# Attention head of a fused attention and SwiGLU kernel: the fourth key block and the tails moved forward, batch 1's casts and batch 0's check moved between engines

## The chip, the cores and the metric

The kernel runs on one core of a Trainium2 chip. The core has five engines that work side by side, each in its own program order: TensorE (matrix products, PE in the profile, with its weight loads as PEld), VectorE (DVE), ScalarE (ACT), GpSimd (POOL) and SyncE (SP), which here only issues transfers. They wait for one another through semaphores. Matrix products land in PSUM, a small memory of eight banks; everything else lives in SBUF. Transfers run on 16 DMA engines and are issued from the queues of SP, ACT and POOL.

The metric is the device time of one execution in microseconds (us): the median over runs. Beside it there is one profiled execution, whose span runs from its first instruction to its last.

## The reference

Eight batches of eight heads, 576 positions, 64 numbers per head. Attention is causal, with a decay that is a cumulative sum; its output is turned into 4608 rows of 512 and goes through RMS norm and a SwiGLU feed-forward with 1536 hidden columns.

```python
s_pos = np.maximum(s, 0.0)
cum = np.cumsum(s_pos, axis=-1)
bias = -(cum[:, :, :, None] - cum[:, :, None, :])
scores = np.where(causal, -1000000000.0, scale * q @ k.T + np.minimum(bias, 0.0))
attn = softmax(scores)                     # exp(scores - max), divided by the sum
x = (attn @ v).transpose(0, 2, 1, 3).reshape(4608, 512)

xn = x / sqrt(mean(x * x) + 1e-6) * rms_g
g = xn @ w_gate
out = (g * sigmoid(g) * (xn @ w_val)) @ w_out
```

## The kernel before

**Banded attention.** The decay is so strong that a query sees only its own block of 128 keys and the block before it; the rest falls under a bound. The kernel computes that band and checks on the side that this was allowed: check_mag (L368) takes the magnitudes of a batch's cast K or Q into `mag`, check_max (L373) folds them in two halves into a running maximum `acc`. At the very end these and other bounds give a flag; a slow general path stands behind the flag and isn't entered with this data.

**Stages of attention, per batch b.** Names in brackets are used later.

- K and Q come in as fp32 into `kq32` (load_kq L123, and load_kq_tail L129 for positions 512 to 575, the "tail"). w is 0 for K and 1 for Q. They are cast to bf16 into `kqn` (cast L135; quarter r of the positions, quarter 4 is the tail). From batch 2 on other ways are used as well.
- t_step (L180) transposes one head pair hp of K or Q on TensorE, four products into a PSUM tile, and copies it to `kqT` by ScalarE or VectorE. tail_step (L194) does the tails of all head pairs.
- s_step (L225) makes scores of key block kb (0 to 4) for the four heads of group g (0 or 1): S(kb, g), or S(b, kb, g). Four products on TensorE, four exponentials on ScalarE (L274) into a slot of `E`, and a causal mask on GpSimd (L283). Block 3 also needs the tail's queries, block 4 the tail alone, for all heads at once.
- av_step (L292) makes AV(qb, g), the output of query block qb: products on TensorE (L300, L306), division by the sum on VectorE (L313, L315), and with g = 1 the sum of squares, on ScalarE (L321) where `act` is set, else on VectorE (L325), then the RMS scale on GpSimd (L328, L331).
- x_scale (L335, instruction L338, VectorE) applies the scale; xt_step (L352) transposes the block on TensorE (L357) and copies it into `xnT` (L364 ScalarE, L366 VectorE). Most later blocks are transposed by DMA instead.

**Feed-forward.** ffn (L658) takes a chunk c of 512 rows, nine in all. Its loop over fb (12 times) does the gate product Gp (L668), the tanh T on ScalarE (L671), the value product Vp (L677), U = (T + 1) * Gp (L680) and Ht = U * Vp (L673; the last one L685) on VectorE. Then come four blocks of 12 output products each (L690). psF is a ring of four PSUM banks that Gp and Vp, some transposes, the score pairs pairF and the output products share; psS, psAV and psT are single tiles.

**Order.** The whole program is written out in order, each engine runs its own part of it strictly in that order, and there are two ways in which the order is made:

- The head (L773 to L884) is written by hand: all of batch 0's attention but its last query block, up to the transposes of its first 512 rows, which make chunk 0. warm(n) (L593) puts n products in that nothing uses.
- From chunk 0 on, step (L599) is called at fixed places of ffn (a slot, counted in `slot`): after each Gp and each Vp, and among the output products. In each slot it puts in at most one piece from each of the side queues (`act_side`, `v_side`, `pool_side`, `dve_side`), then a score step, or a transpose, an AV and a K/Q transpose, as far as lags counted in slots since the pieces that they need allow it (can_t L530, can_s L542, can_av L561). So the order doesn't depend on times; a piece whose data is late makes its engine wait. In chunk 0 the slots hold batch 1's casts, its transposes of K and Q (do_t L489), batch 0's last block, and batch 1's scores and outputs. During the output products of chunk 0 the query blocks (1,1) to (1,3) of batch 1 are finished; (1,3) is transposed on TensorE before chunk 1 begins.

The lines that the change touches: `when` in check (L421) says in which slots batch 0's check runs; do_t (L496) which engine copies batch 1's transposes; L784 clears the part of the E slots that S(3, g) doesn't write; L828 to L880 are the hand-written order of the head; L881 to L884 batch 0's check of Q; L886 to L894 the queues with batch 1's casts; L903 the queue with batch 0's check of K.

Of the kernel before, what the change touches and what calls it, by code (L numbers as in the profile page):

```python
# [26 lines left out]
def kernel(  # L27
# [12 lines left out]
    nc = tc.nc  # L40
# [340 lines left out]
    slot = [0]  # L381
    first, chunk = [0], [0]
    done = {}
# [34 lines left out]
    def check(b, ws=(1, 0)):  # L418
        t = slot[0] + (8 if b >= KB else 0)

        def when(w):  # L421
            if b < 2:
                return slot[0] % 2 and chunk[0] == b
            return phase() >= 25 and slot[0] >= t and (w == 0 or ready(0, "cast", b, 1))
        dve_side.extend((lambda w=w: when(w), f) for w in (ws if b < KB else (0, 1)) for f in (
            lambda w=w: check_mag(b, w), lambda: check_max(0), lambda: check_max(1),
            lambda w=w: done.__setitem__(("check", b, w), slot[0])))
# [61 lines left out]
    def do_t(key, **kw):  # L489
# [5 lines left out]
        else:  # L495
            if b == 1:  # L496
                kw["dve"] = w == 1 and hp > 1
# [273 lines left out]
    with tc.manual_schedule():  # L771
# [12 lines left out]
        nc.gpsimd.memset(E[:, 6:8, :, 192:256], 0.0)  # L784
# [45 lines left out]
        s_first(1, 0, pairF())  # L830
        load_w(moe_w_val, wv_sb, 0)
# [5 lines left out]
        for w in (0, 1):  # L837
            cast(POOL, 0, w, 4, 5)
# [3 lines left out]
        s_first(0, 1, pairF())  # L842
        do_av((0, 1, 0), psT32())
        s_first(1, 1)
        tail_step(0)
        done["T", 0] = 0
        load_v(0, 4)
        do_av((0, 2, 0))
        s_first(2, 1, pairF())
        s30 = do_s((0, 3, 0))  # L850
        s30(False)
        s31 = do_s((0, 3, 1), pairF())
        s31(False)
        do_av((0, 0, 1), psT32())

# [4 lines left out]
        s30.mask()  # L860
        s31.mask()
        do_av((0, 1, 1), act=True)
        do_av((0, 2, 1), psT32(), act=True)
        warm(4)
        x_scale(0, 0)
        do_av((0, 3, 0))
# [14 lines left out]
        check_mag(0, 1)  # L881
        check_max(0)
        check_max(1)
        done["check", 0, 1] = 0  # L884

        def done_cast(w):  # L886
            done["cast", 1, w] = slot[0]
        later(act_side, 1, [lambda r=r: cast(ACT, 1, 0, r, r + 1) for r in range(4)])
        later(pool_side, 1, [lambda: cast(POOL, 1, 0, 4, 5)])
        later(pool_side, 3, [lambda: done_cast(0)])  # L890
        later(pool_side, 4, [lambda: cast(POOL, 1, 1, 2, 3),
                             lambda: (cast(POOL, 1, 1, 3, 4), done_cast(1)),
                             lambda: cast(POOL, 1, 1, 4, 5)])
        later(dve_side, 3, [lambda r=r: cast(DVE, 1, 1, r, r + 1) for r in (0, 1)])  # L894
# [8 lines left out]
        check(0, (0,))  # L903
# [195 lines left out]
```

## Time and profile before

| | us |
|---|---|
| median of three runs (375.37, 375.38, 375.68) | 375.38 |
| profiled execution, whole | 374.85 |
| its span | 373.2 |
| TensorE busy in it | 347.1 (93%) |
| VectorE busy | 279.6 (75%) |
| ScalarE busy | 240.0 (64%) |
| GpSimd busy | 175.2 (47%) |
| first gate product of chunk 0 starts at | 31.85 |
| first gate product of chunk 1 starts at | 76.10 |

How to read what is quoted from the profile: in a timeline, a row has the start and length in us, the engine, the line of the kernel, the operation, what it writes and reads with shapes, how many instructions the row holds, and in brackets how long the engine stood idle before it and what ended that. A row of waits has engine, tile and line, what it waited for, and then us in total, times, longest. A row of windows has the stretch, its length, then for each engine the busy time and in brackets the instructions, then the granted TensorE clock (1.00 is full speed), the busy share of the DMA engines and GB/s. Lengths of neighbouring instructions on one engine overlap a little, so the distance from start to start is up to 0.1 us shorter than the length.

### The profile page before, as it was taken

Reading aid. Unit: us, or ns where it says so; the run is one execution under the profiler, and the core shown is the slowest. Engines: PE = TensorE matmul, PEld = TensorE weight load, DVE = VectorE, ACT = ScalarE, POOL = GpSimd, SP = SyncE. Lnnn points to the kernel's source line nnn. Section 1 sums busy time; section 2 is a strip of 40 time slices with the busy share of each in tenths; the row PEclk is TensorE's granted clock in tenths of the full one; section 3 lists DMA queues with packets and bytes.
Section 4 is the critical chain, followed back from the end, with each engine's and each line's share of the span. In section 5 each row is a group of like instructions: output and inputs, shape, how many; then the busy total and the mean of one; then the engine's idle time right before and its main releaser. Section 6 shows DMA issues by size and latency. Waiting matters only on the chain. (4 is left out here: it accounts for less than half of the span.)

```text
span 373.2 us, 6936 instructions
## 1 busy us (share of the span) xinstructions
PE 347.1 (93%) x2356; PEld 161.4 (43%) x2356; DVE 279.6 (75%) x525; ACT 240.0 (64%) x626; POOL 175.2 (47%) x277
## 2 busy tenths in 40 slices
PE   1777899899999999899999999999999999999993
PEld 1443444454444444444444444444444444444441
DVE  6778988589887878788889897795488548837730
ACT  3787787547877597776778776777677644323321
POOL 5866734974846565779856825523322310000000
PEclk9879999999999999999999999999999999999998
DMA  7999999799997599959999997973310230020012
GB/s 228 192 206 262 148 208 210 122 201 222 127 204 104 52 200 161 159 56 204 147 166 223 139 118 151 122 56 44 99 23 14 44 105 3 0 84 31 0 42 78
DMA packets 125626, 46.22 MB, mean 124 GB/s; under 512 B 104912, under 2 KB 120784, under 8 KB 125584
## 3 DMA queue, kind: packets, MB, share of 16 engines
q0 software_dynamic: 59920, 11.80, 43.9%
q1 hardware_dynamic: 53040, 24.33, 34.7%
q10 hardware_dynamic: 12624, 9.59, 10.2%
q8 instruction: 20, 0.33, 0.4%
q14 instruction: 22, 0.18, 0.2%
HBM read 38.16 MB, written 9.44 MB: 128 GB/s over the span
## 5 line engine op out<-in xcount | busy, mean ns | idle before, releaser
L274 ACT ACTIVATE E<-psS,biasK 128x256 bf16<-128x256 f32 (+3 forms) x352 | 115.1, 416 | 19.7 <-PE psS L250 18.0
L668 PE MATMUL psF<-xnT,wg_sb 128*128 128x512 bf16 x432 | 111.1, 379 | 1.9 <-DMA xnT<-xs_sb 0.8
L677 PE MATMUL psF<-xnT,wv_sb 128*128 128x512 bf16 x432 | 111.1, 379 | 0.1
L690 PE MATMUL psF<-wout_sb,Ht 128*128 128x512 bf16 x432 | 102.3, 379 | 0.0
L283 POOL TENSOR_SCALAR_AFFINE_SELECT E<-E 128x512 bf16<-128x512 bf16 x72 | 51.9, 721 | 92.8 <-ACT E L274 92.0
L671 ACT ACTIVATE T<-psF 128x512 f32<-128x512 f32 x108 | 64.4, 598 | 41.5 <-PE psF L668 38.3
L680 DVE SCALAR_TENSOR_TENSOR U<-T,psF 128x512 bf16<-128x512 f32 x108 | 73.6, 682 | 21.8 <-ACT T L671 21.8
L673 DVE TENSOR_TENSOR Ht<-U,psF 128x512 bf16<-128x512 bf16 x99 | 67.7, 684 | 7.5 <-PE psS L250 0.5
L668 PEld LDWEIGHTS <-wg_sb 128*128 128x128 bf16 x432 | 38.7, 98 | 46.3 <-issue 7.5
L677 PEld LDWEIGHTS <-wv_sb 128*128 128x128 bf16 x432 | 38.6, 98 | 42.8 <-issue 4.6
L690 PEld LDWEIGHTS <-Ht 128*128 128x128 bf16 x432 | 38.7, 98 | 42.0 <-issue 2.3
L338 DVE SCALAR_TENSOR_TENSOR xs_sb<-x_sb,al_all,g_row 128x512 bf16<-128x512 bf16 (+1 forms) x40 | 32.4, 810 | 16.6 <-POOL al_all L331 15.0
L695 ACT ACTIVATE osb<-psF 128x512 f32<-128x512 f32 x36 | 21.4, 595 | 33.7 <-PE psF L690 29.3
L321 ACT ACTIVATE xs_sb<-x_sb 128x512 bf16<-128x512 bf16 (+1 forms) x36 | 22.9, 640 | 21.3 <-DVE x_sb L315 21.2
L175 POOL DMA_DIRECT2D v_sb<-in_v_dram x40 | 35.3, 883 | 0.4 <-issue 0.3
L375 DVE TENSOR_TENSOR acc<-acc,mag 128x1280 bf16<-128x1280 bf16 x32 | 29.5, 936 | 0.4
L250 PE MATMUL psS<-kqT 64*128 64x256 bf16 (+2 forms) x304 | 26.6, 260 | 1.4 <-ACT E L274 1.2
L306 PEld LDWEIGHTS <-E 128*128 128x128 bf16 x320 | 22.5, 99 | 12.1 <-POOL E L283 2.2
L328 POOL TENSOR_SCALAR al_all<-ss_all 128x1 f32<-128x1 f32 (+1 forms) x40 | 11.3, 282 | 27.6 <-ACT xs_sb L321 21.5
L300 PEld LDWEIGHTS <-E 128*128 128x128 bf16 x256 | 20.7, 99 | 8.0 <-DVE x_sb L315 0.8
L331 POOL TENSOR_TENSOR al_all<-al_all,mhalf 128x1 f32<-128x1 f32 (+1 forms) x40 | 22.6, 565 | 3.3
L250 PEld LDWEIGHTS <-kqT 64*128 64x128 bf16 x320 | 10.5, 96 | 29.9 <-issue 28.5
(94 smaller groups left out, 279.7 us busy)
## 6 DMA issues: line engine op xcount, KB each, us to landing
out_dram<-osb SPq DMA_DIRECT2D x36, 256.0 KB, 2.3
kq<-in_q_dram ACTq DMA_DIRECT2D x6, 1024.0 KB, 9.5
v_sb<-in_v_dram POOLq DMA_DIRECT2D x32, 128.0 KB, 7.2
kq<-in_k_dram ACTq DMA_DIRECT2D x2, 1024.0 KB, 10.6
kqn<-in_k_dram POOLq DMA_DIRECT2D x16, 128.0 KB, 4.9
wg_sb<-in_moe_w_gate_dram POOLq DMA_DIRECT2D x2, 768.0 KB, 7.3
wv_sb<-in_moe_w_val_dram POOLq DMA_DIRECT2D x2, 768.0 KB, 10.1
wout_sb<-in_moe_w_out_dram POOLq DMA_DIRECT2D x1, 1536.0 KB, 14.1
```

Source lines behind the costliest of these rows:

```text
L175: nc.gpsimd.dma_start(out=v_sb[0:n, b % 2, c, :, 0:64], in_=v[b, :, c * 128:c * 128 + n, :].rearrange("h p d -> p h d"))
L250: nc.tensor.matmul(pair[par][:, j * W:j * W + M], lhsT=kT, rhs=qT, start=(j == 0), stop=(j == nj - 1))
L274: nc.scalar.activation(out=eo, in_=ei, func=AF.Exp, scale=0.125, bias=biasK[:, kb, bh:bh + 1])
L283: nc.gpsimd.affine_select(out=Ev[:, :, 0:nq], in_=Ev[:, :, 0:nq], pattern=[[0, nh], [1, nq]], compare_op=ALU.is_ge, fill=0.0, base=0, chan ...
L338: nc.vector.scalar_tensor_tensor(out=xs_sb[0:n, (b * NSC + qb) % NX, :], in0=x_sb[0:n, (b * NSC + qb) % NX, :], scalar=al_all[0:n, col:col ...
L375: nc.vector.tensor_tensor(out=acc[:, sl], in0=acc[:, sl], in1=mag[:, sl], op=ALU.max)
L668: nc.tensor.matmul(Gp, lhsT=wg_sb[:, cc, fs], rhs=xnT[:, cc, x0:x0 + DM], start=(cc == 0), stop=(cc == CC - 1))
L671: nc.scalar.activation(out=T, in_=Gp, func=AF.Tanh, scale=0.5)
L673: nc.vector.tensor_tensor(out=Ht[:, fb - 1, :], in0=pend[0], in1=pend[1], op=ALU.mult)
L677: nc.tensor.matmul(Vp, lhsT=wv_sb[:, cc, fs], rhs=xnT[:, cc, x0:x0 + DM], start=(cc == 0), stop=(cc == CC - 1))
L680: nc.vector.scalar_tensor_tensor(out=U, in0=T, scalar=1.0, in1=Gp, op0=ALU.add, op1=ALU.mult)
L690: nc.tensor.matmul(Op, lhsT=Ht[:, fb, tb * 128:(tb + 1) * 128], rhs=wout_sb[:, fb, :], start=(fb == 0), stop=(fb == FB - 1))
```

## The change

In the head, S(3, 0) is computed as the fourth score step, directly behind S(2, 0) and ahead of all scores of group 1; for that the tails' casts go to a place right behind S(1, 0) on GpSimd, ahead of the second weight load, and tail_step goes in front of S(3, 0). The third and later score steps change their PSUM tiles with it, and the two masks of block 3 follow their exponentials instead of standing further down. E's clearing goes to slots 3 and 7. Batch 1's K and Q loads are issued behind AV(1, 0), three score steps earlier. AV(3, 0) stands ahead of AV(1, 1). AV(1, 1) loses `act`, so its squares are summed by VectorE. warm(4) is left out.

Batch 1's casts: of K, quarters 0 and 1 stay on ScalarE and quarters 2 and 3 go to VectorE in one piece, in slot 1; all four quarters of Q go to VectorE as two pairs (they were two on VectorE, two on GpSimd). Q's tail is cast two slots later on GpSimd. All of batch 1's Q transposes are copied by VectorE, where the first two head pairs were copied by ScalarE.

Batch 0's check of Q no longer stands at the end of the head; the checks of Q and K both go through the side queue, at odd slots from 9 on.

```diff
             if b < 2:
-                return slot[0] % 2 and chunk[0] == b
+                return slot[0] % 2 and chunk[0] == b and slot[0] >= 9
...
             if b == 1:
-                kw["dve"] = w == 1 and hp > 1
+                kw["dve"] = w == 1
...
-        nc.gpsimd.memset(E[:, 6:8, :, 192:256], 0.0)
+        nc.gpsimd.memset(E[:, 3, :, 192:256], 0.0)
+        nc.gpsimd.memset(E[:, 7, :, 192:256], 0.0)
...
         s_first(0, 0)
         load_v(0, 3)
         s_first(1, 0, pairF())
+        for w in (0, 1):
+            cast(POOL, 0, w, 4, 5)
         load_w(moe_w_val, wv_sb, 0)
         do_t((0, 2, 0), pT=psT(), dve=True)
         do_t((0, 3, 0), pT=psF16(), dve=True)
         for r in range(4):
             piece(1, 1, r, DVE)
         s_first(2, 0)
-        for w in (0, 1):
-            cast(POOL, 0, w, 4, 5)
+        tail_step(0)
+        done["T", 0] = 0
+        s_first(3, 0, pairF())
         do_t((0, 2, 1), pT=psT(), dve=True)
         do_t((0, 3, 1), pT=psF16(), dve=True)
         do_av((0, 0, 0))
-        s_first(0, 1, pairF())
+        s_first(0, 1)
         do_av((0, 1, 0), psT32())
-        s_first(1, 1)
-        tail_step(0)
-        done["T", 0] = 0
-        load_v(0, 4)
-        do_av((0, 2, 0))
-        s_first(2, 1, pairF())
-        s30 = do_s((0, 3, 0))
-        s30(False)
-        s31 = do_s((0, 3, 1), pairF())
-        s31(False)
-        do_av((0, 0, 1), psT32())
-
         for w in (0, 1):
             nc.vector.memset(kq32[0:1, w, 0, 0:1], 0.0)
             load_kq(nc.sync, 1, w)
             load_kq_tail(nc.sync, 1, w)
-        s30.mask()
-        s31.mask()
-        do_av((0, 1, 1), act=True)
-        do_av((0, 2, 1), psT32(), act=True)
-        warm(4)
+        s_first(1, 1, pairF())
+        load_v(0, 4)
+        do_av((0, 2, 0))
+        s_first(2, 1)
+        do_av((0, 0, 1), psT32())
+        s31 = do_s((0, 3, 1), pairF())
+        s31()
+        do_av((0, 3, 0))
+        do_av((0, 1, 1), psT32())
+        do_av((0, 2, 1), act=True)
         x_scale(0, 0)
-        do_av((0, 3, 0))
         warm(2)
         do_av((0, 3, 1), psT32(), act=True)
...
         do_xt((0, 3), psF16())
-        check_mag(0, 1)
-        check_max(0)
-        check_max(1)
-        done["check", 0, 1] = 0
...
-        later(act_side, 1, [lambda r=r: cast(ACT, 1, 0, r, r + 1) for r in range(4)])
+
+        def pair(w, r):
+            cast(DVE, 1, w, r, r + 1)
+            cast(DVE, 1, w, r + 1, r + 2)
+        later(act_side, 1, [lambda r=r: cast(ACT, 1, 0, r, r + 1) for r in (0, 1)])
         later(pool_side, 1, [lambda: cast(POOL, 1, 0, 4, 5)])
-        later(pool_side, 3, [lambda: done_cast(0)])
-        later(pool_side, 4, [lambda: cast(POOL, 1, 1, 2, 3),
-                             lambda: (cast(POOL, 1, 1, 3, 4), done_cast(1)),
-                             lambda: cast(POOL, 1, 1, 4, 5)])
-        later(dve_side, 3, [lambda r=r: cast(DVE, 1, 1, r, r + 1) for r in (0, 1)])
+        later(dve_side, 1, [lambda: (pair(0, 2), done_cast(0))])
+        later(dve_side, 4, [lambda: pair(1, 0), lambda: (pair(1, 2), done_cast(1))])
+        later(pool_side, 6, [lambda: cast(POOL, 1, 1, 4, 5)])
...
-        check(0, (0,))
+        check(0)
```

## The prediction

> **What bounds the kernel now.** I read the page first (TensorE busy 93% of the span, so what counts is where it is not), then TensorE's waits by stretch, then the timelines of all engines up to the start of chunk 1, because the program order of the changed kernel equals the old one on every engine from there on. All edits lie before the 76 us mark.
>
> TensorE's waits between 32 and 62 us, which is nearly chunk 0's gate and value loop (engine, line, what it waited for: us, times, longest):
>
> ```profile
> PE psT L184 <- ACT kqn L139: 1.1, 1, 1.1
> PE psF L668 <- ACT xnT L364: 0.7, 1, 0.7
> PE psT L184 <- POOL kqn L141: 0.5, 1, 0.5
> PE psS L250 <- ACT E L274: 0.3, 1, 0.3
> ```
>
> The two L184 rows, 1.6 us, are transposes of batch 1's K and Q that wait for casts. The change goes for them, but they are not all that holds this stage. Busy time in the same loop, of all engines from the first gate matmul, and of VectorE from the loop's first U to its last Ht:
>
> ```profile
> 31.85:61.93 30.08, 28.11 (x216) 13.47 (x216) 26.98 (x50) 23.85 (x57) 14.68 (x21) 1.00 1.27 195
> 34.04:63.41 29.37, 26.20 (x50) 1.00 1.27 194
> ```
>
> TensorE is idle for 2.0 us and VectorE (26.20 of 29.37) for 3.2. So VectorE has about 3 us to spare here. What follows shows who sets the restart after chunk 0 (start us, length us):
>
> ```profile
> 62.81 0.69 DVE L685 TENSOR_TENSOR Ht<-U,psF 128x512 bf16<-128x512 bf16 x1
> 64.08 0.69 DVE L325 SCALAR_TENSOR_TENSOR xs_sb<-x_sb 128x512 bf16<-128x512 bf16 x1
> 64.88 0.19 POOL L328 TENSOR_SCALAR al_all<-ss_all 128x1 f32<-128x1 f32 x1 [0.90 <-DVE rZ L313]
> 71.84 0.18 POOL L328 TENSOR_SCALAR al_all<-ss_all 128x1 f32<-128x1 f32 x1
> 72.11 0.57 POOL L331 TENSOR_TENSOR al_all<-al_all,mhalf 128x1 f32<-128x1 f32 x1
> 72.71 1.13 DVE L338 SCALAR_TENSOR_TENSOR xs_sb<-x_sb,al_all,g_row 128x512 bf16<-128x512 bf16 x1 [1.07 <-POOL al_all L331]
> 73.90 0.40 PE L357 MATMUL psT<-ident_bf,xs_sb 128*128 128x128 bf16 x4 [1.50 <-DVE xs_sb L338]
> ```
>
> VectorE's last Ht is followed in its queue by the square of block (1,1) (L325). GpSimd waits 0.90 us for that square, and from 64.88 to 72.68 it has under 0.2 us of gaps (scales, casts of batch 2, a mask, V loads). Its last scale frees L338, and that frees the transpose for which TensorE stands still for 1.50 us. So the restart at 73.90 hangs on VectorE's end of the loop, one to one, and not on TensorE's. After it TensorE is busy in nearly every slice, so a shift there is a shift of the end.
>
> **The change, part by part.** Head first. Its old end:
>
> ```profile
> 29.96 0.75 DVE L338 SCALAR_TENSOR_TENSOR xs_sb<-x_sb,al_all,g_row 128x512 bf16<-128x512 bf16 x1 [0.71 <-POOL al_all L331]
> 30.77 0.40 PE L357 MATMUL psF<-ident_bf,xs_sb 128*128 128x128 bf16 x4 [0.64 <-DVE xs_sb L338]
> 31.85 1.02 PE L668 MATMUL psF<-xnT,wg_sb 128*128 128x512 bf16 x4 [0.69 <-ACT xnT L364]
> ```
>
> 1. The tail casts go ahead of the second weight load and of the mask of S(2,0) on GpSimd: after the mask at 14.61 they run 15.2 to 16.35 (two took 1.15). Q's tail landed at 13.1 (issued 3.98, 9.1 to landing). The weight load is issued 1.2 us later; it took 10.0 and lands near 26.5, before its first use near 33, so it costs nothing; if batch 1's loads beside it cost it another 6 us, the value matmul would wait. V's tail load is issued 3 us later and has 15 us.
>
> 2. tail_step now stands right behind S(2,0) (13.09) in TensorE's queue, so TensorE waits until 16.4 for those casts. Behind it wait the transposes (2,1) and (3,1), ready from 14 to 15.5, and S(0,1). The eight tail transposes (1.0) end at 17.0, the two copies (0.29, 0.28) at 17.55, S(3,0) (0.53) at 18.1, the two head transposes at 18.9, their copies (0.69 each, 0.60 apart) at 19.85, the last half of S(0,1) at 20.3. It was at 17.48. So the exponentials of S(0,1) start 2.9 us later, but ScalarE has done S(3,0) meanwhile (from 18.2, 1.4).
>
> 3. ScalarE then goes through: three sets at 1.45 apart and one of 1.38 from 20.35 end at 26.1 (they ended at 24.95). GpSimd: mask of S(2,1) 24.8 to 25.45, scale 0 (0.8), mask of S(3,1) 26.25 to 26.9. AV(3,1) at 26.95 (was 26.33).
>
> 4. VectorE gets the square of block 1 (L325, 0.69 alone, 1.17 beside a mask), which ScalarE did in an idle stretch: AV(0,1) from 22.9, square 0 at 23.55, AV(3,0) 24.6, AV(1,1) 25.15, square 1 25.8, AV(2,1) 26.6, x_scale 27.15, AV(3,1) 27.85 to 28.45. Then square 3 on ScalarE to 29.2, scale 3 on GpSimd at 29.25 (0.85 to 1.4, the old ones took 0.83 and 1.38), L338 at 30.1 to 30.65. The old way from that instruction to the first gate matmul was 1.89, so the FFN starts at 32.0 to 32.55. I take 32.2, **+0.35**. Ends: -0.6 if the mask before it goes first and the square is 0.69; +1.2 if both are stretched.
>
> 5. warm(4) goes: 0.87 us of TensorE inside a stretch where it waits for masks, nothing by itself (its cover is that wait).
>
> 6. The K and Q loads of batch 1 are issued by SP behind AV(1,0)'s division, near 21.3 instead of 23.88; nothing else is queued on SP, and K (5.5 to landing) and Q (8.1) are there by 27 and 31. So the casts no longer wait for data. Later landing by 3 us would still be in time.
>
> Then the loop. The two cast waits (1.6 us of TensorE) go: ScalarE keeps two K casts behind the first T, VectorE does two K casts ahead of its first U, while it waits for the first gate matmul anyway (cost nothing, cover 1.6 us; a 128x512 cast took 0.42, and 128x256 casts beside GpSimd's DMA issues stretched from 0.28 to 0.80, so at most about 2). What is late next is VectorE. Added between first U and last Ht, by start-to-start distances: two more Q casts (0.33 each) 0.7; transposed Q of heads 0 to 3 copied by VectorE instead of ScalarE, two at 0.60: 1.2; batch 0's check of Q, which had stood ahead of the first U (3.41 us from 30.63, of which 2.2 after the gate matmul started), now with the K check at odd slots from 9.
>
> VectorE's instructions there, added up by distance: 12 U and 12 Ht at 0.60, 14.4; casts 1.35; four copies 2.4; five divisions with two squares 4.55; two x_scales 1.4; two small copies 0.4; two magnitudes (0.82 alone, 1.11 beside GpSimd work) at 0.85, 1.7; four maxima (0.74 distance alone, 1.25 beside GpSimd's casts) at 0.82, 3.3. Sum **29.5**; all alone 28.9, all slow 30.9. I take the value near the lower end because GpSimd's own casts there are halved and masks take a quarter of its time. The same sum for the old order is 25.65 (busy 26.2).
>
> U cannot start before gate matmul (1.05) plus T (0.60): 1.7 after the FFN's start. Two waits stay before saturation: the second U for the second T, behind two ScalarE casts (0.55), the third U for the third T, behind eight exponentials and two copies (0.65). After that TensorE is throttled by its four psF buffers, which VectorE frees, and VectorE has no idle time. So start to end of the last Ht is 1.7 + 1.2 + 29.5 = 32.4 plus 0.1 of the last one's tail, against 63.50 - 31.85 = 31.65: **+0.85** (ends -0.3 with 28.9 and half the waits, +2.3 with 30.9). The cast waits' 1.6 us is thus gained on an engine that then waits for buffers.
>
> Sum: 0.35 + 0.85 = +1.2 at the last Ht, at GpSimd's scale and at the restart. The profiled execution took 374.85 (span 373.2, 1.65 around it), giving 376.05; the median of the three timed runs is 0.53 above it, so **376.6 us**.
>
> [...] The granted clock was 0.50 in 15.88:19.29 and 1.00 again from 22.7, 6.8 us in all, behind a stretch (12.47:15.88) in which TensorE was busy 1.59 of 3.41 us; stretches with 2.1 to 2.3 busy kept the full clock. [...]
>
> **The rivals.**
> (a) Clock. TensorE reaches the transpose of (1,3) no later than now, so its wait there grows from 1.5 to about 2.5 us. If that falls inside one window, about 0.9 of 3.4 busy is less than the 1.59 that lost the clock in the head. One window of 3.41 at half clock delays back-to-back matmuls by 1.7: 378.3. Against: two windows may share the wait.
> (b) Faster. VectorE's spare 3.2 us takes the new work. It decides at a VectorE loop of under 28 us behind the first U, waits included: then the 1.6 of cast waits stays gained, and with the head +0.35 it is 375.4 - 1.25 = 374.1. For it: two waits of 1.0 and 0.5 on VectorE came from TensorE's stalls. Against: 28.9 is the floor.
> (c) Cancels. Head at the -0.6 end and 28.9 in the loop: within 0.7 of 375.4. For it: L338 and the scale are short when undisturbed.
> (d) Head worse: the start of the FFN above 33, because scale 3 and its L338 stretch each other as at 28.5, or the second weight half lands late: 377.7.
>
> **How the numbers follow.** Forecast (slower by 1.2, within 0.9 of it) 0.45, (a) 0.15, (b) 0.12, (c) 0.16, (d) 0.12. A measurement here can tell about 0.2%, 0.75 us. Slower: (a), (d) and nine tenths of the forecast, 0.67; faster: 0.12; within 0.2%: 0.21. The range leaves out most of (b) below and the joint ends above: 374.6 to 378.6; the forecast's own is 375.7 to 377.5.
>
> **What would show it.** TensorE's wait at the tail transposes from 13.5 to about 16.4 and exponentials of S(0,1) near 20.3; first gate matmul near 32.2; no L184 wait for casts in the loop, and in their place TensorE waits at L668, L677 or L184 for U or Ht of VectorE; VectorE idle under 1.5 us between first U and last Ht; last Ht ending near 64.7; the transpose of (1,3) near 75.1 after a longer wait. Wrong if the last Ht ends before 63.5, or if GpSimd's scale of (1,3) does not move with the square of (1,1).

## The result, and the profile after

The changed kernel took 380.09 us (median of six, 378.24 to 381.46), the kernel before 375.39 (374.67 to 375.68) beside it. The ratio is 1.012, with a 95% interval of 1.0092 to 1.0148: **slower by 4.7 us**, in the direction that was forecast, at four times the size, and outside the range. The profiled execution took 379.79 us with a span of 378.1. The stages in the two profiled executions, in us:

| | before | after | shift | forecast |
|---|---|---|---|---|
| exponentials of S(0,1) start | 17.48 | 20.64 | +3.16 | +2.9 |
| last exponential of batch 0's S(3,1) ends | 24.95 | 26.37 | +1.42 | +1.15 |
| last x_scale (L338) of the head starts | 29.96 | 31.99 | +2.03 | +0.14 to 0.69 |
| first gate product | 31.85 | 33.88 | **+2.03** | **+0.35** |
| last Ht of chunk 0 ends | 63.50 | 66.82 | +3.32 | +1.2 |
| loop (first gate to end of last Ht) | 31.65 | 32.94 | **+1.29** | **+0.85** |
| transpose of (1,3), the restart | 73.90 | 77.22 | +3.32 | +1.2 |
| last chunk's first gate product | 336.01 | 340.41 | +4.40 | +1.2 |
| span | 373.2 | 378.1 | +4.9 | +1.2 |

TensorE's waits up to 32 us, between 32 and 62, and between 62 and 85 (engine, tile and line, what it waited for: us, times, longest), of the changed kernel. The rows for 32 to 62 answer to those shown of before:

```profile
PE psT L200 <- POOL kqn L141: 2.3, 1, 2.3
...
PE psF L668 <- ACT xnT L364: 0.7, 1, 0.7
PE psF L668 <- DVE Ht L673: 0.4, 1, 0.4
PE psS L250 <- ACT E L274: 0.3, 1, 0.3
PE psF L357 <- DVE xs_sb L338: 0.3, 1, 0.3
...
PE psT L357 <- DVE xs_sb L338: 2.3, 1, 2.3
```

The two waits for casts (1.6 us) are gone, as intended. A wait of 2.3 us at the tail's transposes is new, the ring of psF buffers now waits for VectorE's Ht, and the wait at the restart has grown from 1.5 to 2.3.

Busy time by engine from the first U to the last Ht (length; PE, PEld, DVE, ACT, POOL; granted clock, DMA share, GB/s):

```profile
35.57:66.74 31.17, 30.06 (x232) 14.15 (x230) 29.98 (x57) 22.98 (x58) 13.61 (x19) 1.00 1.14 191
```

VectorE is busy 29.98 of 31.17 us, where it was 26.20 of 29.37. Its spare time has gone from 3.2 to 1.2 us: it is the loop's bound now.

The chain behind the loop (start, length, engine, line, operation):

```profile
66.13 0.69 DVE L685 TENSOR_TENSOR Ht<-U,psF 128x512 bf16<-128x512 bf16 x1
...
67.41 0.69 DVE L325 SCALAR_TENSOR_TENSOR xs_sb<-x_sb 128x512 bf16<-128x512 bf16 x1
...
75.16 0.18 POOL L328 TENSOR_SCALAR al_all<-ss_all 128x1 f32<-128x1 f32 x1
75.43 0.57 POOL L331 TENSOR_TENSOR al_all<-al_all,mhalf 128x1 f32<-128x1 f32 x1
76.03 1.13 DVE L338 SCALAR_TENSOR_TENSOR xs_sb<-x_sb,al_all,g_row 128x512 bf16<-128x512 bf16 x1 [1.07 <-POOL al_all L331]
77.22 0.40 PE L357 MATMUL psT<-ident_bf,xs_sb 128*128 128x128 bf16 x4 [2.29 <-DVE xs_sb L338]
```

From the end of the last Ht (66.82) to the restart it is 10.40 us. Before it was also 10.40 (63.50 to 73.90): the same chain, passed on one to one.

The head's end, GpSimd and VectorE of the changed kernel:

```profile
26.19 1.00 POOL L331 TENSOR_TENSOR al_all<-al_all,mhalf 128x1 f32<-128x1 f32 x1
27.16 0.62 POOL L283 TENSOR_SCALAR_AFFINE_SELECT E<-E 128x512 bf16<-128x512 bf16 x1
27.87 0.51 POOL L328 TENSOR_SCALAR al_all<-ss_all 128x1 f32<-128x1 f32 x1
28.46 0.56 POOL L331 TENSOR_TENSOR al_all<-al_all,mhalf 128x1 f32<-128x1 f32 x1
29.10 0.75 POOL L328 TENSOR_SCALAR al_all<-ss_all 128x1 f32<-128x1 f32 x1
29.94 0.55 POOL L331 TENSOR_TENSOR al_all<-al_all,mhalf 128x1 f32<-128x1 f32 x1
30.57 0.75 POOL L328 TENSOR_SCALAR al_all<-ss_all 128x1 f32<-128x1 f32 x1
31.41 0.55 POOL L331 TENSOR_TENSOR al_all<-al_all,mhalf 128x1 f32<-128x1 f32 x1
...
29.05 0.75 DVE L338 SCALAR_TENSOR_TENSOR xs_sb<-x_sb,al_all,g_row 128x512 bf16<-128x512 bf16 x1
30.52 0.75 DVE L338 SCALAR_TENSOR_TENSOR xs_sb<-x_sb,al_all,g_row 128x512 bf16<-128x512 bf16 x1 [0.71 <-POOL al_all L331]
31.99 0.75 DVE L338 SCALAR_TENSOR_TENSOR xs_sb<-x_sb,al_all,g_row 128x512 bf16<-128x512 bf16 x1 [0.71 <-POOL al_all L331]
...
33.88 1.02 PE L668 MATMUL psF<-xnT,wg_sb 128*128 128x512 bf16 x4 [0.69 <-ACT xnT L364]
```

The mask of S(3,1) (L283 at 27.16) stands behind the first scale and ahead of the other three. These then alternate with L338: the scale that comes beside a running L338 takes 0.75 us instead of 0.19, L331 follows it, and only then can the next L338 start. Each round takes 1.47 us (29.05, 30.52, 31.99). ScalarE's square of block 3 started at 29.12 and its sum was read out at 29.84; the scale that uses it started at 30.57. The kernel before had only one such round. One round earlier its scale came just ahead of the L338 and was short:

```profile
27.28 0.19 POOL L328 TENSOR_SCALAR al_all<-ss_all 128x1 f32<-128x1 f32 x1
28.50 0.75 DVE L338 SCALAR_TENSOR_TENSOR xs_sb<-x_sb,al_all,g_row 128x512 bf16<-128x512 bf16 x1 [0.44 <-POOL al_all L331]
28.55 0.75 POOL L328 TENSOR_SCALAR al_all<-ss_all 128x1 f32<-128x1 f32 x1
```

### The profile page after: what moved, and what is told of

It reads as the page before. It is cut to its first block, busy times and chain, and to the rows that moved or that the text cites. A ratio compares the mean times of both kernels' runs of the same rounds, so it can differ in the third digit from the quotient of the medians.

```text
span 378.1 us, 6927 instructions
## 1 busy us (share of the span) xinstructions
PE 350.9 (93%) x2352; PEld 162.2 (43%) x2352; DVE 283.0 (75%) x533; ACT 236.6 (63%) x620; POOL 175.6 (46%) x276
## 5 line engine op out<-in xcount | busy, mean ns | idle before, releaser
L668 PE MATMUL psF<-xnT,wg_sb 128*128 128x512 bf16 x432 | 111.1, 379 | 3.4 <-DMA xnT<-xs_sb 1.7
L677 PE MATMUL psF<-xnT,wv_sb 128*128 128x512 bf16 x432 | 111.0, 379 | 0.1
L283 POOL TENSOR_SCALAR_AFFINE_SELECT E<-E 128x512 bf16<-128x512 bf16 x72 | 52.3, 727 | 93.4 <-ACT E L274 92.8
L668 PEld LDWEIGHTS <-wg_sb 128*128 128x128 bf16 x432 | 38.8, 98 | 48.4 <-issue 8.7
L677 PEld LDWEIGHTS <-wv_sb 128*128 128x128 bf16 x432 | 38.7, 98 | 43.1 <-issue 4.6
L338 DVE SCALAR_TENSOR_TENSOR xs_sb<-x_sb,al_all,g_row 128x512 bf16<-128x512 bf16 (+1 forms) x40 | 33.2, 830 | 17.6 <-POOL al_all L331 15.2
L695 ACT ACTIVATE osb<-psF 128x512 f32<-128x512 f32 x36 | 21.4, 594 | 35.4 <-PE psF L690 30.3
L175 POOL DMA_DIRECT2D v_sb<-in_v_dram x40 | 35.1, 878 | 1.9 <-PE psF L668 1.7
L375 DVE TENSOR_TENSOR acc<-acc,mag 128x1280 bf16<-128x1280 bf16 x32 | 29.1, 920 | 0.3
L250 PE MATMUL psS<-kqT 64*128 64x256 bf16 (+2 forms) x304 | 27.0, 262 | 1.4 <-ACT E L274 0.9
L328 POOL TENSOR_SCALAR al_all<-ss_all 128x1 f32<-128x1 f32 (+1 forms) x40 | 13.3, 332 | 29.5 <-ACT xs_sb L321 20.1
L331 POOL TENSOR_TENSOR al_all<-al_all,mhalf 128x1 f32<-128x1 f32 (+1 forms) x40 | 22.7, 566 | 3.3
L250 PEld LDWEIGHTS <-kqT 64*128 64x128 bf16 x320 | 10.1, 96 | 30.2 <-issue 28.8
```

The lines of the kernel that those rows point to most:

```text
L175: nc.gpsimd.dma_start(out=v_sb[0:n, b % 2, c, :, 0:64], in_=v[b, :, c * 128:c * 128 + n, :].rearrange("h p d -> p h d"))
L250: nc.tensor.matmul(pair[par][:, j * W:j * W + M], lhsT=kT, rhs=qT, start=(j == 0), stop=(j == nj - 1))
L283: nc.gpsimd.affine_select(out=Ev[:, :, 0:nq], in_=Ev[:, :, 0:nq], pattern=[[0, nh], [1, nq]], compare_op=ALU.is_ge, fill=0.0, base=0, chan ...
L338: nc.vector.scalar_tensor_tensor(out=xs_sb[0:n, (b * NSC + qb) % NX, :], in0=x_sb[0:n, (b * NSC + qb) % NX, :], scalar=al_all[0:n, col:col ...
L375: nc.vector.tensor_tensor(out=acc[:, sl], in0=acc[:, sl], in1=mag[:, sl], op=ALU.max)
L668: nc.tensor.matmul(Gp, lhsT=wg_sb[:, cc, fs], rhs=xnT[:, cc, x0:x0 + DM], start=(cc == 0), stop=(cc == CC - 1))
```

## The experiments

The expectations name their theories by letters where they use them. The two that matter are **D**: VectorE's work sets chunk 0's loop, and GpSimd's chain passes its end on to the restart one to one; and **C**: the head's slow TensorE clock is what costs. All times in the table but the medians are of profiled executions, in us; "last stretch" is restart to the end of the span. A profiled execution need not be a typical one: those of e2_loop (378.15) and e5_fill (379.83) were the slowest of their kernels, those of e7_gaps (376.98) and e9_square (378.64) the second slowest, and the loops of these last two hold a window of 3.41 us at half clock.

| run | first gate | loop | last Ht to restart | restart | last stretch | median | ratio to before, 95% |
|---|---|---|---|---|---|---|---|
| e1_head | 33.72 | 31.57 | 10.40 | 75.69 | 299.8 | 377.60 | 1.0048 to 1.0085 |
| e2_loop | 31.51 | 32.94 | 10.40 | 74.85 | 301.7 | 377.10 | 1.0031 to 1.0065 |
| e3_warm | 33.18 | 32.94 | 10.40 | 76.52 | 301.2 | 380.84 | 1.0134 to 1.0170 |
| e4_nocheck | 33.88 | 29.86 | 10.39 | 74.13 | 300.2 | 375.89 | 1.0005 to 1.0032 |
| e5_fill | 33.92 | 32.94 | 10.40 | 77.26 | 300.9 | 378.32 | 1.0052 to 1.0089 |
| e6_tail | 32.79 | 32.96 | 10.42 | 76.17 | 299.9 | 377.71 | 1.0046 to 1.0092 |
| e5_qact | 33.85 | 30.84 | 10.41 | 75.10 | 301.2 | 377.75 | 1.0037 to 1.0072 |
| e7_gaps | 32.40 | 32.78 | 10.42 | 75.60 | 299.8 | 375.40 | 0.9987 to 1.0021 |
| e8_ksplit | 31.87 | 31.70 | 10.41 | 73.98 | 299.6 | 375.26 | 0.9994 to 1.0016 |
| e10_casts | 31.77 | 30.93 | 10.41 | 73.11 | 299.9 | 375.01 | 0.9983 to 1.0006 |
| e9_square | 32.32 | 34.63 | 10.41 | 77.36 | 299.6 | 377.70 | 1.0038 to 1.0083 |
| e11_best | 32.27 | 30.87 | 10.41 | 73.55 | 299.3 | 374.75 | 0.9982 to 1.0016 |

### The head alone, and the loop alone

The first takes the head of the changed kernel (tails, score steps, masks, E's clearing) and keeps the loop's side queues and batch 0's check of Q at the end of the head as before. The second is the opposite half:

```diff
 # e2_loop, against the kernel before (its head is left as it was)
-                return slot[0] % 2 and chunk[0] == b
+                return slot[0] % 2 and chunk[0] == b and slot[0] >= 9
...
-                kw["dve"] = w == 1 and hp > 1
+                kw["dve"] = w == 1
...
-        check_mag(0, 1)
-        check_max(0)
-        check_max(1)
-        done["check", 0, 1] = 0
...
-        check(0, (0,))
+        check(0)
```

(and batch 1's casts as in the changed kernel.)

> Only the head of the change (order of batch 0's scores and tails, loads, warm products); batch 1's casts, the Q copies and batch 0's check are as in the kernel before, the check of Q again at the end of the head. Theory H (the head's new order makes the masks and with them GpSimd's chain of RMS scales late): first gate product near 33.9 as in the changed kernel (31.85 before), the loop as long as before (31.65 from there to the end of the last Ht), so the restart at the transpose of (1,3) near 76.0 and 377 to 378 in all, about +2. Theory L (the loop's part makes nearly all of the loss, the head's delay is absorbed): 375.5 to 376.

> Only the loop's part (casts on VectorE in pairs, all Q copies by VectorE, batch 0's check from slot 9 on); the head in the order of before, without the check of Q at its end. Theory D (VectorE has no spare time in chunk 0's loop and the restart hangs on its end): first gate near 31.9, first U about 1.7 later, VectorE idle under 1.5 us in the loop, loop 32.9 long as in the changed kernel, restart near 75.2, 376.5 to 377. Rival (the loop is longer only because the head left its work behind; the two cast waits of 1.6 us are gained): loop about 30, 373.8 to 374.5.

The head alone puts the first gate product at 33.72, +1.87, and leaves the loop at 31.57. The loop alone leaves the head (31.51; it is 0.34 early already at its first L338, 24.40 against 24.74, for a reason that I did not follow) and gives 32.94, to the digit what the changed kernel has. So the two halves are nearly independent, and the head is the bigger one: +1.87 to +2.03 there against +1.29 in the loop. Both halves lose more in the median (2.4 and 1.9) than at the restart (1.79 and 0.95). The profiled execution of the second shows one way in which that happens. This is TensorE's clock right behind the restart of the loop-alone run, against that of the changed kernel in the same place (columns as above):

```profile
75.35:78.76 3.41, 3.41 (x17) 1.49 (x16) 0.36 (x1) 0.23 (x1) 3.40 (x6) 0.50 1.04 158
```

```profile
77.22:80.63 3.41, 3.41 (x26) 1.85 (x27) 1.40 (x4) 0.74 (x2) 3.40 (x6) 1.00 0.90 156
```

In the loop-alone run, the window behind the longer wait ran at half clock; chunk 1 came 4.30 us behind the restart and not 2.20 as before. That is rival (a).

### A busier TensorE in the head's wait

```diff
         s_first(2, 0)
+        wps = psAV()
+        for _ in range(12):
+            nc.tensor.matmul(wps, lhsT=ident_bf, start=True, stop=True,
+                             rhs=kqn[:, 0, 0, 0].rearrange("p h d -> p (h d)"))
         tail_step(0)
...
         do_av((0, 2, 1), act=True)
+        warm(4)
         x_scale(0, 0)
```

> The changed kernel with twelve unused products of 512 columns in the wait ahead of tail_step, on the bank psAV, and warm(4) back behind AV(2,1): it puts activity where TensorE stood idle and changes nothing on the other engines. Theory C (the half clock, which the changed kernel's profile shows up to 32 us, makes the head late): full clock from 16 to 18 us on, first gate at 32.8 or earlier, 1 to 2 us off the total: 378 to 379. Theory H (the head is late by the chain of exponentials, masks and scales): clock full earlier, but first gate within 0.5 us of 33.9 and the total within 0.6 of the changed kernel's 380.

In the changed kernel the profile has no clock record ahead of 32.02, and its unused 512-column products at 26 to 32 us took 616 ns on average, against 379 in the kernel before and 0.63 us (L677 at 33.98) in the window of e9_square that was granted 0.50: the head ran at half clock (the profile's clock figure counts time without a record as full speed; it gives 1.00 for 12 to 31 us). With 12 products in the wait the clock was full from 11.99, ahead of the products, to 22.23, and half from there to 29.06. The first gate product came 0.7 us earlier, at 33.18, between the 32.8 of theory C and the 33.4 of theory H. The median did not fall, but it says little about the head: in this profile the restart lost the clock (chunk 1 came 4.10 us behind it). The 0.7 is also not a strict bound, since the four products of warm(4) ran at half clock there and held AV(3,1) back from the mask's end at 26.89 to 27.92.

Three other profiles bear on it. In e8_ksplit the head is that of the kernel before, and it too ran slow: its unused products from 23 to 27 us took 628 ns, and the full clock came at 27.00. Its first gate product is at 31.87, as before. In e5_fill, with the head of the changed kernel, the full clock came at 29.70 instead of 32.02, and the first gate product at 33.92. And e9_square below, at half clock until 28.91, has it at 32.32, by its order alone. So theory C is not the head's main cause. What holds the head's end is the chain of GpSimd and VectorE; its last round took 1.47 us at half clock and 1.46 in e5_fill at full clock.

### Batch 0's check left out

```diff
-        check(0)
+        done["check", 0, 0] = done["check", 0, 1] = 0
```

> The changed kernel without batch 0's check (two magnitudes and four maxima, 4.9 us of VectorE in chunk 0's loop, are left out, so one guard of the fast path is not computed). Theory D: the loop is shorter by 2.5 to 4.5 us (until TensorE's own 28 to 29 bind), the restart comes earlier by the same, and the total falls to 376 to 377.5. Rival (the loop's end does not set the restart): under 1 us, 379 to 380.

Two magnitudes and four maxima took 0.81 to 1.25 us each in the changed kernel. Without them the loop is 29.86, shorter by 3.08, and the restart is 3.09 earlier with the same head. TensorE's waits of this run between 32 and 62 us, and VectorE's largest:

```profile
PE psF L668 <- ACT xnT L364: 0.7, 1, 0.7
PE psS L250 <- ACT E L274: 0.3, 1, 0.3
```

```profile
DVE U L680 <- ACT T L671: 2.5, 3, 1.5
```

VectorE waits again, and TensorE no longer waits for it. Theory D holds: in the changed kernel VectorE sets the loop, and what the loop lost came out at the restart. It lost less than the 4.9 us of the check, because VectorE is then no longer what sets it.

### Unused products in front of the restart

```diff
         b, qb = key
+        if key == (1, 3):
+            wps = psT32()
+            for _ in range(9):
+                nc.tensor.matmul(wps, lhsT=ident_bf, rhs=wg_sb[:, 0, 0:DM], start=True, stop=True)
         xt_step(b, qb, pX)
```

> The changed kernel with nine unused products (about 2 us) put directly ahead of the transpose of block (1,3), where TensorE stands still for 2.3 us. Theory A (in part of the runs this wait costs the clock, about 2 us each time, as the two profiles of the loop's part and of the warm products show it): no half clock behind the restart in the profile, chunk 1 starts 2.2 us behind the restart, the runs lie closer together, median near 379, against 380.1 of the changed kernel. Rival (the spread has another source): median and spread as in the changed kernel, 378.2 to 381.5.

The products fill the wait and move nothing: the restart stays at 77.26. Still the median falls by 1.8 us, from 380.09 to 378.32, and the spread from 3.2 to 2.1 us.

The profiles taken together show what such a wait costs and how often. Six of the fourteen have a wait of 2.28 to 2.30 us at the restart. In three (e2_loop, e3_warm, e5_qact) the half clock followed, and chunk 1 came 4.30, 4.10 and 3.65 us behind the restart; in the changed kernel, e6_tail and e9_square the clock stayed full, and it was 2.20 to 2.41. None of the six profiles with a wait of 1.50 to 1.52, and neither of the two with the products, lost the clock there. So rival (a), priced at 1.7 us in the prediction, costs 1.2 to 2.1, and it falls due in part of the executions, not in the profiled one of the changed kernel.

The granted clock averaged over a whole run doesn't tell which executions paid it. In the changed kernel three of the six runs had 0.998 to 0.999 (378.24, 378.68, 379.79), and three had 0.976 to 0.990 (380.39, 380.56, 381.46); but the profile of e1_head has 0.975 with its half clock in the head and none behind the restart. That the three slower runs lost the clock at the restart is likely and not shown.

### The tails put back behind S(0,1)

```diff
         s_first(2, 0)
-        tail_step(0)
-        done["T", 0] = 0
-        s_first(3, 0, pairF())
         do_t((0, 2, 1), pT=psT(), dve=True)
         do_t((0, 3, 1), pT=psF16(), dve=True)
         do_av((0, 0, 0))
-        s_first(0, 1)
+        s_first(0, 1, pairF())
+        tail_step(0)
+        done["T", 0] = 0
+        s_first(3, 0)
```

(E is cleared in slot 4 and not in 3, since the order of the score steps sets the slots.)

> The changed kernel with tail_step and S(3,0) behind S(0,1) instead of ahead of the transposes of heads 4 to 7; the tails are still cast early. Theory H1 (TensorE's wait for the tail casts and all that stands behind it makes the exponentials, the masks and with them the scales late): exponentials of S(0,1) at 17.6 again, the last of them end near 24.5 instead of 26.4, first gate product at 32.0 or earlier, restart 1.5 to 2 us earlier, total near 378. Theory H2 (VectorE's extra square and the order of GpSimd's scales make the head late whatever the scores do): first gate still above 33.2.

The exponentials of S(0,1) start at 17.67 again, the last ones end at 25.28, and the first gate product comes at 32.79. That is between the 32.0 of H1 and the 33.2 of H2: both share in it. 1.09 of the head's 2.03 us comes from the tails and S(3,0) standing ahead of the transposes, with the wait for the tail casts. The loop is unchanged (32.96). 0.94 us of the head's loss is left.

### The first two Q copies back on ScalarE

```diff
-                kw["dve"] = w == 1
+                kw["dve"] = w == 1 and hp > 1
```

> The changed kernel with Q's first two head pairs copied by ScalarE again, 1.2 us less of VectorE in the loop and 1.2 more of ScalarE. Theory D (VectorE bound): loop 31.7 to 32.0 instead of 32.94, restart earlier by 0.9 to 1.2, total 378.8 to 379.2. Rival (ScalarE's queue is as full): loop 32.6 or longer, total as in the changed kernel.

The two copies were to bring 1.2 us, two at 0.60. The loop lost 2.10. The restart came 2.12 earlier, the median fell by 2.3. From the first U to the last Ht (columns as above):

```profile
35.54:64.61 29.07, 28.46 (x226) 13.95 (x230) 27.89 (x54) 24.06 (x60) 13.85 (x19) 1.00 1.27 204
```

VectorE's busy time accounts for all of it: 29.98 became 27.89, and its idle time stayed at 1.2. Besides the two copies, one maximum (L375) took 0.81 instead of 1.25 and one x_scale (L338) 0.75 instead of 1.21. In the changed kernel both ran beside a mask of GpSimd (51.51 and 64.25). They meet a mask here too, but now the mask is the stretched one (1.10 and 1.00 where it takes 0.63 in other places).

### Batch 0's check in the head's gaps

```diff
         do_av((0, 1, 0), psT32())
+        check_mag(0, 0)
         s_first(1, 1)
...
         do_av((0, 2, 0))
+        check_max(0)
         s_first(2, 1, pairF())
...
         x_scale(0, 2)
+        check_max(1)
+        done["check", 0, 0] = 0
         do_xt((0, 2), psF16())
```

(Against the kernel before. Besides, Q's two maxima go into the loop at odd slots from 5, and K's quarters 2 and 3 are cast by VectorE in slot 1.)

> The kernel before with three edits that follow from theory D: batch 0's check of K stands in gaps of VectorE in the head instead of in the loop, two of the four K casts of batch 1 go from ScalarE to VectorE, and the maxima of the Q check go into the loop, the magnitude stays at the head's end. In the loop VectorE has 1.4 to 2 us less. Theory D: first gate within 0.3 of 31.85, loop 29.7 to 30.5 (31.65 before), restart 1 to 2 us earlier than 73.9, total 373.6 to 374.6. Rival (the cast waits of TensorE, not VectorE, set the loop's end): the wait for ScalarE's casts goes, about 1.1 earlier with the same VectorE idle time as before; (no gain) within 0.2% of the kernel before if the head becomes later by what the loop gains.

Level with before: 375.40, ratio 0.9987 to 1.0021. The first gate product came 0.55 later, because the maximum behind x_scale(0, 2) stands in the chain of scales and L338 (the last L338 at 30.51 and not 29.96), and the loop took 32.78, far from the 29.7 to 30.5 of theory D. This profile had the half clock in the loop's first full window:

```profile
33.03:36.44 3.41, 3.19 (x8) 1.22 (x8) 2.77 (x5) 1.63 (x3) 1.62 (x3) 0.50 1.14 199
```

At the price of such a window, 1.7 us, the loop would have taken about 31.1 (an estimate). VectorE was idle for 5.4 us of it, so it did not set this loop. TensorE's cast wait did not go; it passed to the next cast, GpSimd's (1.2 us). Theory D describes the changed kernel, where VectorE is full, and not this one.

### Batch 1's casts alone

```diff
 # e8_ksplit, against the kernel before; e10_casts has these lines too
-        later(act_side, 1, [lambda r=r: cast(ACT, 1, 0, r, r + 1) for r in range(4)])
+        later(act_side, 1, [lambda r=r: cast(ACT, 1, 0, r, r + 1) for r in (0, 1)])
-        later(pool_side, 3, [lambda: done_cast(0)])
+        later(dve_side, 1, [lambda: (cast(DVE, 1, 0, 2, 3), cast(DVE, 1, 0, 3, 4), done_cast(0))])
 # e10_casts besides: Q's quarters as in the changed kernel
-        later(pool_side, 4, [lambda: cast(POOL, 1, 1, 2, 3),
-                             lambda: (cast(POOL, 1, 1, 3, 4), done_cast(1)),
-                             lambda: cast(POOL, 1, 1, 4, 5)])
-        later(dve_side, 3, [lambda r=r: cast(DVE, 1, 1, r, r + 1) for r in (0, 1)])
+        later(dve_side, 4, [lambda: (cast(DVE, 1, 1, 0, 1), cast(DVE, 1, 1, 1, 2)),
+                            lambda: (cast(DVE, 1, 1, 2, 3), cast(DVE, 1, 1, 3, 4), done_cast(1))])
+        later(pool_side, 6, [lambda: cast(POOL, 1, 1, 4, 5)])
```

> The kernel before with one edit: quarters 2 and 3 of batch 1's K are cast by VectorE in slot 1 and not by ScalarE. Theory D (VectorE sets chunk 0's loop once its spare is used up): before had 3.2 us of spare on VectorE between first U and last Ht; the two casts take about 0.7 of it, and 0.7 more come ahead of the first U, so the wait of 1.1 us of TensorE for the cast goes but little is gained: loop 31.2 to 31.6 (before 31.65), restart 73.5 to 73.9, median 374.9 to 375.4. Rival B (the waits for casts are what holds the loop): loop 30.5, restart 72.8, median 374.2.

> The kernel before with all of the change's casts of batch 1 (K quarters 2 and 3 and all four quarters of Q on VectorE, Q's tail two slots later on GpSimd) and nothing else: batch 0's check and the copies stay as they were before. Theory D: VectorE's work between first U and last Ht is 26.2 + 0.7 (two more Q casts) and its start is 0.7 later; both waits for casts of TensorE (1.6 us) go: loop 31.6 to 32.3, restart 73.9 to 74.5, median 375.4 to 376.0. Rival B: loop 30.0, restart 72.3, median 373.8.

With K's split alone the loop is 31.70 and the median that of before. The number is close to theory D's 31.2 to 31.6, but its reason doesn't hold: what took the gain was not VectorE's load but the next cast in line, as this row of TensorE's timeline shows (idle time and what ended it in brackets):

```profile
40.86 0.23 PE L184 MATMUL psT<-ident_bf,kqn 128*128 128x128 bf16 x1 [1.25 <-POOL kqn L141]
```

With all casts moved, neither theory had it: the loop is 30.93, between D's 31.6 to 32.3 and the rival's 30.0. TensorE then has no cast wait (1.6 before), and of that 0.72 arrives at the end of the loop. The restart is at 73.11, 0.79 earlier, but the median gains 0.13, which is nothing that can be measured (0.9983 to 1.0006). The trace shows part of where it went: chunk 4 starts 0.42 earlier only, behind a wait of 0.42 us for exponentials (L250 for E, at 192.48) that the kernel before doesn't have. What delays those exponentials I have not settled.

### The square of block (0,1), and the parts put together

```diff
 # e9_square: e6_tail and
-        do_av((0, 1, 1), psT32())
+        do_av((0, 1, 1), psT32(), act=True)
 # e11_best: e9_square, with the edits of e5_qact and e5_fill
```

> The changed kernel with the tails and S(3,0) behind S(0,1) (as in the run with the tails put back) and besides the square of AV(1,1) on ScalarE again. If what is left of the head's loss (first gate matmul at 32.79 there, 31.85 before) comes from VectorE's extra square in front of the scales: first gate matmul at 31.9 to 32.2, restart 75.3 to 75.6, median 376.9. If it comes from the two masks of block 3 standing in front of and between GpSimd's scales: first gate matmul stays at 32.6 to 32.8, restart at 76.0, median 377.6. The loop is 32.9 either way.

> As the run before, and in addition the first two pairs of batch 1's Q transposes are copied by ScalarE again and nine unused products of 512 columns stand in front of the transpose of (1,3). Theory D and the clock rival together: the head as in the run before (first gate matmul near 32.0, or 32.7), loop 30.84 as in the run with the copies on ScalarE, so restart 73.2 to 73.9, full clock there, restart to end of span 299.9: span 373.2 to 373.8, median 374.9 to 375.5, level with before. If the copies' gain of 2.1 us depends on the later head: loop 31.5 to 32, median 376.

With the square on ScalarE the first gate product is at 32.32, 0.47 earlier: between the two cases, half of the 0.94 us that was left. The trace shows how: with the square gone from VectorE, the first scale's L331 took 0.57 instead of 0.99, and the mask behind it began at 25.59 instead of 26.06. The other 0.47 lies in the second L338 (27.50, before 27.32) and in the round behind it (1.46, before 1.18). I put it down to the two masks of block 3 among the scales; no run takes them away alone. The loop came out at 34.63 and not at 32.9: in this execution its first window had the half clock.

```profile
32.32:35.73 3.41, 3.41 (x9) 1.17 (x9) 0.87 (x2) 1.51 (x3) 2.10 (x3) 0.50 1.10 180
```

34.63 - 32.94 = 1.69 is half of 3.41: one such window costs what the prediction took for it.

All put together give a loop of 30.87, as with the copies on ScalarE, and a restart at 73.55. The median is 374.75, but the ratio is 0.9982 to 1.0016: level. Three of the twelve runs lie at 376.2 to 377.0, each with a mean granted clock of 0.975 or 0.976, the other nine at 374.06 to 374.93 with 0.983 to 0.999. So what the casts and the later check bring is about what the head, still 0.42 late, takes, and no version of this study beats the kernel before by more than can be measured.

## Why the prediction was wrong

**Step 1** (tail casts 15.2 to 16.35) and **step 2** held. The casts ran from 15.23 to 16.54. TensorE waited 2.3 us, the transposes began at 15.98 and S(0,1)'s exponentials at 20.64 (20.35 forecast).

**Step 3** held to 0.3: the exponentials ended at 26.37 (26.1). The mask of S(3,1) is already off, 27.16 and not 26.25. The mask of S(2,1) ahead of it came 0.4 later than forecast (25.20), and the first scale with it; its L331 took 1.00 beside VectorE's square (0.57 in the quiet places), where the whole scale had been counted as 0.8.

**Step 4 is the step that failed.** It followed one path, the last square to scale 3 to L338, and let scale 3 start as soon as ScalarE's square was done, at 29.25. The square was done at 29.84, but scale 3 started at 30.57: GpSimd was still on scale 2, which had come late behind the mask and beside an L338. The step added +0.35 with an upper end of +1.2; the run has **+2.03**. Of the 1.68 us between the 32.2 that was taken and 33.88, 0.59 is the late square (behind the late mask of step 3), 0.73 is scale 3 standing in GpSimd's queue behind scale 2, and 0.36 is the way from scale 3 to L338, 1.42 where 1.06 was taken. The last piece, 1.89 from L338 to the first gate product, was exact (31.99 to 33.88). Against the kernel before, 1.09 of the 2.03 is the tails' new place (e6_tail), 0.47 the square that VectorE got (e9_square), and 0.47 is left. The late start of the FFN is rival (d) in place, above 33, and in kind: a scale beside an L338 took 0.75 us and not 0.19, but already a round earlier than (d) has it, and L338 is not stretched by it (0.75 there, 0.74 with GpSimd idle, at 61.37 in the kernel before). I had given it 0.12.

L338 ran from 29.05 to 29.80, and the scale that started at 29.10 ended at 29.85 (0.75), where the one at 25.92, with no L338 beside it, took 0.19; the next pair did the same (30.52 to 31.27, 30.57 to 31.32). Why the scale is stretched is not shown. With its L331 it took 1.39 us both times (29.10 to 30.49, 30.57 to 31.96): that is the upper end of step 4's "0.85 to 1.4", and not for the last scale alone.

**Step 5** (leaving out warm(4) costs nothing by itself) was not contradicted: back in e3_warm, at half clock, it delayed AV(3,1). In the changed kernel's profile the head ran at half clock; by e3_warm the clock's part of the head's loss is about 0.7 us, which would lie within the three shares above. **Step 6** held in its result, no cast waited for data, but not in its times: batch 1's K took 8.6 us to land and Q 11.9, where 5.5 and 8.1 were taken, so Q was there at 35.1 and not at 31.

**The loop.** The mechanism was right, and the sum was 0.44 short. The first U came 1.69 behind the first gate product (1.7 forecast). VectorE was busy for 29.98 us, 3.78 more than before; the forecast sums, 25.65 for the old order and 29.5 for the new, differ by 3.85. So the added work was right. But the old sum of 25.65 stood against 26.20 us busy, and the 0.55 between them was not carried over: 29.5 and 0.55 are 30.05. Single terms missed both ways. The four Q casts held VectorE for 0.67 and 1.14 us from 37.99 and 39.26, 1.81 for a term of 1.35; the divisions with their squares took less than the 4.55 counted. The waits came to 1.19 for 1.2, partly by luck: the trace has one of 0.53, for TensorE, and small gaps, not the two waits that were named. The total is +1.29 for +0.85. Rival (b), a gain because VectorE had time to spare, is refuted by e4_nocheck and e2_loop; with the casts alone (e10_casts) a part of it came, 0.72 us in the loop. Its condition was a VectorE loop below 28 us; the run had 31.2.

**The sum.** The step from the last Ht to the restart, one to one, held in all fourteen profiles (10.39 to 10.42 us). "After it, a shift there is a shift of the end" failed by 1.6: the profile has 299.3 us from the restart to the end before and 300.9 after. TensorE waited for blocks transposed by DMA (L668 for xnT) 0.47 us ahead of chunk 2 and 1.27 ahead of chunk 3, where before had one such wait of 0.78, ahead of chunk 3. The delay of the two chunks' starts grew by 0.61 and 0.49 there. The last 0.5 lies behind ScalarE's last copy of output products (L695, start 367.34 before and 371.74 after): from its start to the end it is 5.9 us before and 6.4 after.

**Rival (a)** came on top in part of the executions: in three of six profiles with such a wait. The wait grew to 2.29 (2.5 forecast). The three that lost the clock had the whole wait inside one window; in the three that kept it a window's border split the wait, as the counterargument to (a) had said. The borders are counted in steps of 3.413 us from a change of the granted clock: such changes lay 6.83 and 348.16 us apart in the kernel before (2 and 102 steps), and 344.75 in the changed kernel (101). This is TensorE in the window that holds the whole wait in the loop-alone run, and in the two that share it in the changed kernel (busy TensorE, granted clock, DMA share, GB/s):

```profile
71.94:75.35 3.41, 1.13 (x9) 1.00 1.12 106
```

```profile
72.98:76.39 3.41, 1.95 (x10) 1.00 1.03 128
76.39:79.80 3.41, 2.58 (x22) 1.00 1.13 179
```

Only the first was followed by a window at half clock. Of the 4.7 us between the medians, 3.3 is what the profile shows at the restart. The other 1.4 is of the size of the waits for transposed blocks and of the lost clock; their shares in the median are not shown.

## What to carry to other kernels

Where two engines hand work back and forth for several blocks, cost the whole alternation and not the last block's path: one late start ahead of it (here a mask in front of three scales) is paid in full, and each round has the price of the two instructions when they meet (1.47 us a round here). VectorE, with 3.2 us to spare of 29.37, took only part of such a move: the casts alone made the loop 0.7 us shorter (e10_casts), casts, copies and check together 1.3 longer (e2_loop). Work moved to it should be taken as a new sum for that engine and set against the other engines' sum before any wait is booked as saved. And a wait that had grown to 2.3 us, about two thirds of a clock window of 3.41, cost 1.2 to 2.1 us besides its length in the three of six profiles where it fell inside one window, and left the clock full in the other three, so one profile doesn't show it.

## What the runs showed of the hardware

- The full clock was lost behind windows of 3.41 us that were not idle. TensorE was busy in the window ahead of a half-clocked one for 1.13 us (e2_loop, and at the same place e3_warm and, with 1.12, e5_qact), and in heads for 0.83 (e4_nocheck), 1.51 (e6_tail), 1.75 (e9_square) and 2.12 (e3_warm). Busy time alone doesn't decide it: at the restart 1.59 (e6_tail), 1.79 (e9_square) and 1.95 (the changed kernel) kept the full clock. What else decides it is not shown.
- The half clock came for one window (3.41 us) at the restart, but the changed kernel's head, with TensorE busy 14.34 of the 19 us from 12 to 31, shows no full clock before 32.02, and the head-alone run had the half clock for 17.07 us from 15.2. In that run windows with up to 3.07 of 3.41 us busy were followed by another at half clock; in the kernel before, 3.12 brought the full clock back.
- Where a maximum (L375) or an L338 of VectorE met a mask of GpSimd, either side could be the stretched one: in the changed kernel a maximum and an L338 took 1.25 and 1.21 us beside masks of 0.78 and 0.63; in e5_qact the same two took 0.81 and 0.75, and the masks beside them 1.10 and 1.00. That is 0.9 of the 2.10 us that this run gained in a loop that VectorE bounds.
